# Attention, low-rank mixing and FFN on one core: batch 1's pooled attention result added inside the mixing, every fourth weight remainder on VectorE, raw weight chunks paced up to 16 ahead

## The chip, the cores and the metric

The kernel runs on one core of a Trainium2 chip. The metric is the device time of one execution in microseconds (us). Shown is the median of three runs, 1007.35 us (1007.11 to 1008.32). The profile is of a further execution, which took 1009.96 us.

## What is computed

Inputs q, k and v are 8 batches × 8 heads × 576 positions × 64, in f32 (the weights are f64). For each head two attentions are added, and the heads' results, side by side, are the x of a mixing and an FFN:

```python
q_d, k_d, v_d = (mean over groups of 4 positions)      # 144 pooled positions
out_up    = repeat(softmax(q_d k_d^T / 8) v_d, 4 times each)      # the pooled ("global") part
out_local = softmax(q k^T / 8, only where |i - j| < 4) v          # the local band
x  = (out_up + out_local), heads side by side          # 576 x 512 for each batch
u  = x + (x^T U V)^T                                   # U 576 x 32, V 32 x 576
out = u + relu(u w1) w2                                # w1 512 x 2048, w2 2048 x 512
```

## The kernel before

**A planner writes the order.** The code first only registers operations (class `Plan`): each has an engine, an estimated duration, the buffers that it reads and writes, and a priority. The planner then plays the schedule through with these estimates and emits the instructions in the order that came out. On the chip every engine runs its own list in that fixed order, and waits by semaphores where data is not there. All transfers are requested by SyncE (SP), also in that order: a request that has to wait holds up all those behind it. So a change of one cost or buffer can move instructions everywhere.

**Attention.** Work goes by batch (b) and head pair (hp), 4 pairs to a batch. Batch 0 has a form of its own at the start. For batches 1 to 7 (28 pairs), `late_global` makes the pooled part: scores, softmax, product with pooled v (`ps_a`, L571), scaled into `od` (L575; 112 rows × 3 × 64). It then stores `od` to `up_s` in DRAM, each row four times (L581, 6 transfers a pair). `local_attn` makes the band: its weights `ms`, products `Pt` of seven neighbours (GpSimd, L837); beside them, as the eighth addend, ScalarE copies the pooled part `ul` (L831), read back from `up_s` (L825); VectorE sums the eight (`acc`, L842); the sum is stored to `x_s` (L844).

**Mixing.** `mix_part` reads the pair's x back in two layouts: `xL` (positions on partitions, L890 and L893), and `Y` (L901), which VectorE transposes to `xT` (L906). ScalarE rounds `xL` to `xH` (L907), GpSimd makes the remainder `xL` (L908). TensorE multiplies with `Ust` (U in two parts) into `ps_hu` (L916). From that ScalarE and VectorE make `stk` (L920, L921, L924), which TensorE multiplies with `Vst` into `ps_u` (L723). VectorE adds it to `xT` (L727); ScalarE and GpSimd split the sum into a rounded part `uH` (L730) and a remainder `uL` (L732).

**FFN.** It goes by tiles of 288 positions (four, batches 0 and 1) and then 384; a tile of batch 1 can begin when all four pairs of that batch are mixed. A tile has 16 steps: 12 matmuls with w1 (`ps_h`, L941), relu split into `hH` (ScalarE, L949) and `hL` (VectorE, L950), and, three steps later, 12 matmuls with w2 into four accumulators (`acc`, L966). Steps before the 19th have only one PSUM bank for `ps_h`, so there a step waits for the `hL` of the one ahead. Steps of the FFN and attention's matmuls alternate on TensorE.

**Weights.** w1 and w2 come as 32 raw f64 chunks (512 KB each; `wr`, L414) and are converted by `convert`: ScalarE takes the upper 16 bits (`half`, L347), VectorE joins the bits (`y`, L350, in a PSUM bank; `c`, L352), ScalarE rounds to `W` (L358), GpSimd makes the remainder (L362). U and V go the same way with the remainder on VectorE (L366). Step 0 of the second product waits for the first 12 chunks (`NA`). The planner requests a chunk once the one `WD` = 4 earlier is converted.

Of the kernel before, what the change touches and what calls it, by code (L numbers as in the profile page):

```python
# [203 lines left out]
def attn_mix_ffn_kernel(ctx: ExitStack, tc, q, kp, vp, qT, kT, v, U, Ub, V, w1, w2, band, eye, pool, vw, ident, outT):  # L204
# [129 lines left out]
    nc.gpsimd.memset(Upool, 0.0)  # L334

    def convert(raw, pp, n, hi_out, lo_out, a, wkey, name, prio, own_bank=False, l0=0):
        t = buf(ffn, [128, CN], I32, name, "cT:" + name, 3)
# [12 lines left out]
        dve(n, lambda: nc.vector.tensor_scalar(  # L350
            out=yi(), in0=h().bitcast(I16)[:pp, :n], scalar1=65536.0, scalar2=None, op0=ALU.mult), [h, t], [y], prio)
        dve(1.15 * n, lambda: nc.vector.scalar_tensor_tensor(  # L352
            ti(), mid(), 13, yi(), op0=ALU.logical_shift_right, op1=ALU.bitwise_or), [raw, y], [t], prio)
# [4 lines left out]
        act(n, lambda: nc.scalar.activation(hi_out(), ta(), AF.Copy, scale=1.0 if big else 256.0), [t], own("H"), prio)  # L358
        if lo_out is None:
            return  # L360
        if big:
            pool_tt(1.0 * n, lambda: nc.gpsimd.tensor_tensor(  # L362
                out=lo_out(), in0=ta()[l0:], in1=hi_out()[l0:].bitcast(F32), op=ALU.subtract),
                [t, *own("H")], own("L"), prio)
        else:
            dve(n, lambda: nc.vector.scalar_tensor_tensor(  # L366
                lo_out(), ta()[l0:], 256.0, hi_out()[l0:].bitcast(F32), op0=ALU.mult, op1=ALU.subtract),
                [t, *own("H")], own("L"), prio)
# [433 lines left out]
    def local_attn(b, hp, up_s, x_s, s_s, prio):  # L802
# [22 lines left out]
        dma(lambda: nc.sync.dma_start(out=ul(), in_=up_s().rearrange("h (c s) d -> (h c) s d", s=NPOS)),  # L825
            [(up_s, 0), (up_s, 1)], [ul], prio + 0.2, 300)
        for p0 in range(0, NPOS, 2):
# [14 lines left out]
            dve(8.5 * n * D, lambda n=n, ps=ps, Pt=Pt: nc.vector.tensor_reduce(  # L842
                out=acc()[:, ps, :], in_=Pt()[:, :n], axis=AX.X, op=ALU.add), [(Pt, 0), (Pt, 1)], [(acc, p0)], prio)
# [245 lines left out]
```

## Time and profile before

| | before |
|---|---|
| median of 3 runs | 1007.35 us |
| profiled execution | 1009.96 us |
| its span, first to last instruction | 1008.2 us |
| mean granted TensorE clock | 0.990 |
| TensorE busy | 973.4 us (97%) |
| VectorE busy | 440.4 us (44%) |
| ScalarE busy | 349.6 us (35%) |
| GpSimd busy | 572.3 us (57%) |

In the rows of the profile PE is TensorE, PEld its weight loads, DVE VectorE, ACT ScalarE, POOL GpSimd and SPq SyncE's queue of requests. L941 is line 941 of the kernel before. A row of a timeline has the start, the duration, engine, line, operation and tiles (out<-in), and in brackets how long the engine had been idle and what ended that. A row of a group has the count, the total, and the mean in ns. The granted clock is 1.00 where TensorE runs at full speed.

### The profile page before, as it was taken

To read this page: it belongs to the slowest core of one execution; us is meant where nothing else is said; L and a number is where in the kernel's file an instruction comes from. 1 tells how busy PE (TensorE), PEld (TensorE's weight loads), DVE (VectorE), ACT (ScalarE), POOL (GpSimd) and SP (SyncE) were. 2 spreads that over 40 slices of the span, in tenths; PEclk is the share of its full clock that TensorE was granted. 3 is DMA by queue.
4 is the path that set the end of the run, shared out by engine and by line. 5 is a ranking of instruction groups with operands and counts; after the bars stand their busy time and mean duration, and the time that the engine had idled before them with its cause. 6 is when DMAs were issued, how large, how long until landed. Compare 5 with 4: busy or idle time off the path is not lost.

```text
span 1008.2 us, 24256 instructions
## 1 busy us (share of the span) xinstructions
PE 973.4 (97%) x9724; PEld 944.7 (94%) x9724; DVE 440.4 (44%) x824; ACT 349.6 (35%) x1023; POOL 572.3 (57%) x641
## 2 busy tenths in 40 slices
PE   5979999799999999999999999999999999999998
PEld 4769899799899999999999999999999999999998
DVE  5666855535453543642635444454363222211211
ACT  5766644333343333432433333433331221111110
POOL 6677897867766764864867866766764111300100
PEclk9989999989999999999999999999999999999999
DMA  9678867656564645655554565465541021000000
GB/s 280 170 243 228 260 147 152 142 129 159 108 152 105 171 92 124 147 129 125 147 129 104 145 150 127 111 161 123 123 121 54 13 68 24 32 1 1 32 1 31
DMA packets 220648, 120.01 MB, mean 119 GB/s; under 512 B 173988, under 2 KB 196856, under 8 KB 220536
## 3 DMA queue, kind: packets, MB, share of 16 engines
q1 hardware_dynamic: 220536, 118.47, 47.2%
q8 instruction: 76, 1.25, 0.5%
q14 instruction: 36, 0.29, 0.1%
HBM read 87.57 MB, written 30.86 MB: 117 GB/s over the span
## 4 chain that ended last, share of the span: by engine, by line
PE 80%; DMA 4%; POOL 4%; DVE 2%; issue 1%; SPq 1%; ACT 1%; DVEq 0%; POOLq 0%
PE ps_h L941 36%; PE acc L966 35%; PE ps_a L571 2%; POOL Pt L837 2%; PE ps_b L775 2%; PE ps_hu L916 2%; DMA ul<-up_s 1%; PE ps_t L556 1%; PE ps_b L768 1%; DMA s_s<-se 1%; DVE acc L842 1%; PE ps_u L723 1%; POOL W L362 1%; DMA gT<-in_kT 1%; SPq L791 1%
## 5 line engine op out<-in xcount | busy, mean ns | idle before, releaser
L966 PE MATMUL acc<-hH,W 128*128 128x384 f32 (+1 forms) x1664 | 441.9, 327 | 0.0
L941 PE MATMUL ps_h<-uH,W 128*128 128x384 f32 (+1 forms) x1376 | 360.4, 324 | 5.3 <-DVE hL L950 5.3
L966 PEld LDWEIGHTS acc<-hH,W 128*128 128x128 f32 x1664 | 297.4, 188 | 2.2
L966 PE MATMUL acc<-hL,W 128*128 128x384 f32 (+1 forms) x832 | 268.2, 322 | 0.0
L837 POOL TENSOR_TENSOR Pt<-vl,ms 128x896 f32<-128x896 f32 (+1 forms) x140 | 239.4, 1789 | 43.9 <-DMA vl<-in_vp 23.9
L950 DVE SCALAR_TENSOR_TENSOR hL<-ps_h,hH 128x384 fp32r<-128x384 f32 (+1 forms) x208 | 109.1, 524 | 342.6 <-ACT hH L949 342.6
L941 PEld LDWEIGHTS ps_h<-uH,W 128*128 128x128 f32 x1376 | 246.4, 190 | 7.5 <-DVE hL L950 6.3
L949 ACT ACTIVATE hH<-ps_h 128x384 fp32r<-128x384 f32 (+1 forms) x208 | 97.2, 467 | 378.3 <-PE ps_h L941 370.3
L941 PE MATMUL ps_h<-uL,W 128*128 128x384 f32 (+1 forms) x688 | 221.6, 322 | 1.4 <-POOL uL L732 1.4
L842 DVE TENSOR_REDUCE acc<-Pt 128x128 f32<-128x1024 f32 (+1 forms) x140 | 152.8, 1107 | 55.0 <-POOL Pt L837 28.0
L966 PEld LDWEIGHTS acc<-hL,W 128*128 128x128 f32 x832 | 156.7, 188 | 0.0
L941 PEld LDWEIGHTS ps_h<-uL,W 128*128 128x128 f32 x688 | 130.8, 190 | 1.6 <-POOL uL L732 1.6
L941 PE MATMUL ps_h<-u,W 128*128 128x384 f32 x432 | 98.1, 334 | 0.0
L831 ACT ACTIVATE Pt<-ul 128x128 f32<-128x128 f32 (+1 forms) x140 | 55.6, 432 | 92.6 <-DVE acc L842 61.7
L908 POOL TENSOR_TENSOR xL<-xL,xH 116x640 fp32r<-116x640 f32 x28 | 44.0, 1570 | 67.1 <-ACT xH L907 55.5
L732 POOL TENSOR_TENSOR uL<-xT,uH 128x384 fp32r<-128x384 f32 (+2 forms) x52 | 40.9, 808 | 68.4 <-ACT uH L730 66.1
L976 POOL TENSOR_TENSOR o<-uH,uL 128x384 f32<-128x384 f32 (+1 forms) x43 | 38.9, 938 | 70.0 <-DMA out_t<-o 70.0
L941 PEld LDWEIGHTS ps_h<-u,W 128*128 128x128 f32 x432 | 76.9, 188 | 0.0
L531 POOL TENSOR_TENSOR vr<-vr 72x256 f32<-72x256 f32 x56 | 41.4, 740 | 31.2 <-DMA vr<-in_v 31.1
L362 POOL TENSOR_TENSOR W<-c,W 128x512 fp32r<-128x512 f32 x32 | 41.1, 1287 | 14.5 <-ACT W L358 14.5
L727 DVE TENSOR_TENSOR xT<-ps_u,xT 128x384 f32<-128x384 f32 (+2 forms) x64 | 27.3, 450 | 32.1 <-PE ps_u L723 31.9
L775 PE MATMUL ps_b<-smk,smq 64*32 64x144 f32 x672 | 38.6, 294 | 0.4 <-POOL smk L439 0.4
(131 smaller groups left out, 903.3 us busy)
## 6 DMA issues: line engine op xcount, KB each, us to landing
wr<-in_W SPq DMA_DIRECT2D x32, 511.8 KB
vl<-in_vp SPq DMA_DIRECT2D x56, 240.0 KB
vr<-in_v SPq DMA_DIRECT2D x64, 144.0 KB
gT<-in_kT SPq DMA_DIRECT2D x28, 291.0 KB
gq<-in_qT SPq DMA_DIRECT2D x28, 288.0 KB
up_s<-od SPq DMA_DIRECT2D x168, 48.0 KB
ul<-up_s SPq DMA_DIRECT2D x28, 288.0 KB
x_s<-acc SPq DMA_DIRECT2D x28, 288.0 KB
```

The costliest lines, as they stand in the source:

```text
L362: pool_tt(1.0 * n, lambda: nc.gpsimd.tensor_tensor(out=lo_out(), in0=ta()[l0:], in1=hi_out()[l0:].bitcast(F32), op=ALU.subtract), [t, *own ...
L531: pool_tt(256, lambda x=x: nc.gpsimd.tensor_tensor(out=x()[:, :, 0:2, :], in0=x()[:, :, 0:2, :], in1=x()[:, :, 2:4, :], op=ALU.add), [x], ...
L732: pool_tt(n, lambda uH=uH, uL=uL, uf=uf, us=us: nc.gpsimd.tensor_tensor(out=uL.ap(hp, us), in0=uf(), in1=uH.ap(hp, us).bitcast(F32), op=AL ...
L775: nc.tensor.matmul(pg()[m:m + QL, a * SD:(a + 1) * SD], sq()[o, n:n + QL], sk()[o], start=True, stop=True)
L831: act(n * D, lambda n=n, ps=ps, Pt=Pt: nc.scalar.activation(Pt()[:, :n, :, 7], ul()[:, ps, :], AF.Copy), [ul], [(Pt, 1)], prio, 0.16)
L837: nc.gpsimd.tensor_tensor(out=Pt()[:, :n, :, 0:7].rearrange("p s d o -> p o s d"), in0=win, in1=at()[:, ps, :].rearrange("p s o -> p o s") ...
L842: dve(8.5 * n * D, lambda n=n, ps=ps, Pt=Pt: nc.vector.tensor_reduce(out=acc()[:, ps, :], in_=Pt()[:, :n], axis=AX.X, op=ALU.add), [(Pt, 0 ...
L908: pool_tt(640, lambda: nc.gpsimd.tensor_tensor(out=xL(), in0=xL().bitcast(F32), in1=xH().bitcast(F32), op=ALU.subtract), [xL, xH], [xL], prio)
L941: nc.tensor.matmul(ps()[:, :tn], W1[fc]()[:, w, dc, :], u.ap(dc), start=(n == 0), stop=(n == 3 * NDC - 1))
L949: last_h[i] = act(tn, lambda: nc.scalar.activation(hH()[:, :tn], ps()[:, :tn], AF.Relu), [ps], [hH], FIRST, 0.05)
L950: dve(tn, lambda: nc.vector.scalar_tensor_tensor(hL()[:, :tn], ps()[:, :tn], 0.0, hH()[:, :tn].bitcast(F32), op0=ALU.max, op1=ALU.subtract ...
L966: nc.tensor.matmul(ac[e]()[:, :tn], W2[fc]()[:, w, es], hx()[:, :tn], start=(fc == 0 and n == 0), stop=(fc == NFC - 1 and n == 2))
```

## The change

It has three parts, and the planner's order follows from them.

1. *Batch 1's pooled part.* For the four pairs of batch 1, `late_global` no longer stores `od`, and `local_attn` no longer reads `ul` nor copies it; its sums have seven addends. `mix_part` gets `od` (in two buffers that alternate) and adds it in the two places where x is used. Into `ps_hu` go six more f32 matmuls, `od` with a new constant `Upl` (U summed over groups of four positions). Six further f32 matmuls transpose `od` with the identity into free columns of the same bank (`oT`), and VectorE adds that to `xT`, each column four times (128 x 576), ahead of `stk`. `Upl` is made once by 12 small matmuls (`l_mm`) and two ScalarE copies.
2. *Remainders.* Of the 32 weight chunks every fourth has its remainder made by VectorE instead of GpSimd (8 chunks).
3. *Requests.* `WD` is 16 instead of 4, and chunk n gets an earliest time of 20 + 2.2 n us in the planner. That is no wait on the chip; it places the request in SyncE's list.

```diff
-    WD = 4
+    WD = 16
+    WAT, WAS = 20, 2.2
...
+    Upl = const.tile([128, 2, NQ, R], F32, name="Upl")
...
+    nc.gpsimd.memset(Upl, 0.0)
...
-        if big:
+        k = len(done) - 1
+        if big and not (k % 4 == 3):
             pool_tt(1.0 * n, lambda: nc.gpsimd.tensor_tensor(
...
-            dve(n, lambda: nc.vector.scalar_tensor_tensor(
-                lo_out(), ta()[l0:], 256.0, hi_out()[l0:].bitcast(F32), op0=ALU.mult, op1=ALU.subtract),
+            dve(1.15 * n, lambda: nc.vector.scalar_tensor_tensor(
+                lo_out(), ta()[l0:], 1.0 if big else 256.0, hi_out()[l0:].bitcast(F32), op0=ALU.mult, op1=ALU.subtract),
...
+        def l_mm():
+            for a in range(NQ):
+                for n, r in enumerate((3 * a // 2, 3 * a // 2 + 1)):
+                    for hh, m in enumerate((64, QC)):
+                        c = 64 - QL * r + QC * a
+                        nc.tensor.matmul(u3()[hh * 64:hh * 64 + m, a], pool_sb()[:, c:c + m], Ublk[:, r, 0:R],
+                                         start=(n == 0), stop=(n == 1))
+        op(PE, 1.0, l_mm, ["UbH", pool_sb], [pl], prio)
...
-            after=done[len(done) - WD:len(done) - WD + 1] if len(done) >= WD else ())
+            after=done[len(done) - WD:len(done) - WD + 1] if len(done) >= WD else (), at=WAT + WAS * len(done))
...
-        od = g([128, NQ, D], "od")
+        od = g([128, NQ, D], "od") if b > 1 or hp % 2 == 0 else buf(loc, [128, NPOS, D], F32, "ul")
...
+        if up_s is None:
+            return s_s, od
...
+        NO = 7 + (up_s is not None)
+        if up_s is not None:
+            ul = lb([128, NPOS, D], "ul")
+            dma(lambda: nc.sync.dma_start(out=ul(), in_=up_s().rearrange("h (c s) d -> (h c) s d", s=NPOS)),
...
-                out=acc()[:, ps, :], in_=Pt()[:, :n], axis=AX.X, op=ALU.add), [(Pt, 0), (Pt, 1)], [(acc, p0)], prio)
+                out=acc()[:, ps, :], in_=Pt()[:, :n, :, 0:NO], axis=AX.X, op=ALU.add), [(Pt, 0), (Pt, 1)], [(acc, p0)], prio)
...
+                for a in range(NQ if od is not None and i == 0 else 0):
+                    for hh in range(2):
+                        nc.tensor.matmul(ph()[:R, hh * D:(hh + 1) * D], Upl[:NP, hh, a], od()[:NP, a], start=False, stop=False)
+            if od is None:
+                return
+            for a in range(NQ):
+                for hh in range(2):
+                    o, m = slice(hh * 64, hh * 64 + QC), slice(hh * D, (hh + 1) * D)
+                    nc.tensor.matmul(oT()[m, a * QC:(a + 1) * QC], od()[o, a], ident_sb[o, o], start=True, stop=True)
...
+            dve(S, lambda: nc.vector.tensor_tensor(
+                out=xT().rearrange("p (j r) -> p j r", r=4), in0=xT().rearrange("p (j r) -> p j r", r=4),
+                in1=oT().unsqueeze(2).broadcast_to([128, SD, 4]), op=ALU.add), [ph, *xk], xk, prio)
...
-                up_s = buf(dram, [2, S, D], F32, "up_s", bufs=6)
+                up_s = buf(dram, [2, S, D], F32, "up_s", bufs=6) if b > 1 else None
```

How the order moves is shown at three places. The first is SyncE's list at the end of batch 1's last pair, before the change; `x_s_3105`, `xL_3189` and `Y_3248` are that pair's, `up_s_3081`, `vl`, `vr` and `ul_3187` belong to batch 2's first pair.

```order
L581 DMA up_s_3081<-od_3074 192x1x64 x3
L844 DMA x_s_3105<-acc_2964 128x576
L581 DMA up_s_3081<-od_3074 192x1x64 x3
L741 DMA vl_3135<-in_vp 64x960 x2
L529 DMA vr_3161<-in_v 72x2x256
L825 DMA ul_3187<-up_s_3081 128x576
L890 DMA xL_3189<-x_s_3105 112x2x320
L893 DMA xL_3189<-x_s_3105 4x2x320
L901 DMA Y_3248<-x_s_3105 32x18x32 x4
```

The same pair after the change (`x_s_3064`, `xL_3139`, `Y_3146`; the lines have moved by some 25):

```order
L764 DMA vl_3033<-in_vp 64x960 x2
L869 DMA x_s_3064<-acc_2865 128x576
L820 DMA sc_3071<-s_s_2957 128x9x7
L915 DMA xL_3139<-x_s_3064 112x2x320
L918 DMA xL_3139<-x_s_3064 4x2x320
L926 DMA Y_3146<-x_s_3064 32x18x32 x4
L604 DMA up_s_3237<-od_3231 192x1x64 x6
```

The loads of x now follow their store with one request between, and the next pair's `up_s` stands behind them. The second place is TensorE at the end of the first FFN tile: before, from the last matmul of step 31 of the second product on.

```order
L966 MATMUL acc3_2411<-hH_3318,W2_15_2269 128x288
L916 MATMUL ps_hu_3400<-xH_3380,Ust_82 64x128 x5
L916 MATMUL ps_hu_3400<-xL_3189,Ust_82 64x128 x5
L723 MATMUL ps_u_3433<-Vst_83,stk_3413 128x288
L723 MATMUL ps_u_3439<-Vst_83,stk_3413 128x288
```

After, from the same matmul on; `ul_2810` is the second of the two buffers that `od` uses.

```order
L1007 MATMUL acc3_2425<-hH_3219,W2_15_2090 128x288
L941 MATMUL ps_hu_3372<-xH_3322,Ust_82 64x128 x5
L945 MATMUL ps_hu_3372<-ul_2810,Upl_84 32x64 x6
L941 MATMUL ps_hu_3372<-xL_3139,Ust_82 64x128 x5
L951 MATMUL ps_hu_3372<-ident_sb_81,ul_2810 64x48 x6
L746 MATMUL ps_u_3409<-Vst_83,stk_3401 128x288
L746 MATMUL ps_u_3411<-Vst_83,stk_3401 128x288
```

The twelve new matmuls stand in the pair's `ps_hu`; the place of `ps_hu` and `ps_u`, next to each other behind step 31, is the same. The third place is VectorE where the FFN begins: before, from the twelfth chunk's join on (`y_a` and `y_h` are the same step in two banks; `hL_1204` is that of step 0, `hL_1295` that of step 1).

```order
L352 SCALAR_TENSOR_TENSOR c2_1115<-wr_1054,y_a_1145 128x512
L350 TENSOR_SCALAR y_h_1163<-half_1158 128x512
L352 SCALAR_TENSOR_TENSOR c1_1157<-wr_1086,y_h_1163 128x512
L350 TENSOR_SCALAR y_h_1192<-half_1170 128x512
L352 SCALAR_TENSOR_TENSOR c2_1169<-wr_1110,y_h_1192 128x512
L950 SCALAR_TENSOR_TENSOR hL_1204<-ps_h_1175,hH_1198 128x288
L350 TENSOR_SCALAR y_h_1236<-half_1224 128x512
L950 SCALAR_TENSOR_TENSOR hL_1295<-ps_h_1207,hH_1234 128x288
```

After (`hL_1207` is that of step 0, `hL_1264` that of step 1; L372 is a remainder on VectorE):

```order
L357 SCALAR_TENSOR_TENSOR c2_1174<-wr_1009,y_a_1195 128x512
L991 SCALAR_TENSOR_TENSOR hL_1207<-ps_h_1179,hH_1200 128x288
L355 TENSOR_SCALAR y_h_1225<-half_1203 128x512
L372 SCALAR_TENSOR_TENSOR W2_3_1210<-c2_1174,W2_3_1210 128x512
L357 SCALAR_TENSOR_TENSOR c1_1202<-wr_1067,y_h_1225 128x512
L355 TENSOR_SCALAR y_h_1252<-half_1237 128x512
L991 SCALAR_TENSOR_TENSOR hL_1264<-ps_h_1212,hH_1250 128x288
```

Two chunks' conversions that stood ahead of step 0's `hL` now stand behind it, with a remainder among them. Earlier in the same list, VectorE's first chunk conversion is its 17th instruction before and its 45th after: it has moved behind pair 1's attention, as the first requests for weights have moved behind the loads of q, k and v of batch 0 in SyncE's list.

More of the change, by code (lines that the diff above doesn't have):

```diff
@@ L264, in psum_pair, with dma @@
         return two
-    def dma(fn, r, w, prio, kb=295.0, issue=0.47, lat=1.3, after=()):
+    def dma(fn, r, w, prio, kb=295.0, issue=0.47, lat=1.3, after=(), at=0.0):
         late = (1.5 if r else 2.0) * (50 <= prio < 80) + 0.75 * (prio >= 80)
-        return op(SP, issue, fn, r, w, prio, after, move=0.01 + kb / 290.0, at=AT if prio >= 35 else 0.0, lat=lat + late)
+        return op(SP, issue, fn, r, w, prio, after, move=0.01 + kb / 290.0, at=max(at, AT if prio >= 35 else 0.0), lat=lat + late)
     def dve(n, fn, r, w, prio, two_x=False, after=()):
@@ L388, in load_ublk @@
         act(2 * R, lambda: nc.scalar.activation(Upool[:QH, :, 0:R], u4(), AF.Copy), [pu], ["Up"], prio, 0.16)
+        pl = psum(ps_acc, "ps_p", "acc1:p", 1)
+        u3 = lambda: pl()[:, :NQ * R].rearrange("p (a r) -> p a r", a=NQ)
+        def l_mm():
[7 more added lines that the diff above has]
+        for hh in range(2):
+            act(NQ * R, lambda o=slice(hh * 64, hh * 64 + QC), hh=hh: nc.scalar.activation(
+                Upl[o, hh], u3()[o], AF.Copy), [pl], [f"Ul{hh}"], prio, 0.16)
     def load_u(prio):
@@ L585, in late_global @@
             dma(lambda hh=hh: store(hh), [od], [(up_s, hh)], prio, 160, 1.3)
-        return s_s
+        return s_s, None
     def load_t(t, src, b, h0, prio):
@@ L830, in local_attn @@
             ps = slice(p0, p0 + n)
-            act(n * D, lambda n=n, ps=ps, Pt=Pt: nc.scalar.activation(
-                Pt()[:, :n, :, 7], ul()[:, ps, :], AF.Copy), [ul], [(Pt, 1)], prio, 0.16)
+            if up_s is not None:
+                act(n * D, lambda n=n, ps=ps, Pt=Pt: nc.scalar.activation(
+                    Pt()[:, :n, :, 7], ul()[:, ps, :], AF.Copy), [ul], [(Pt, 1)], prio, 0.16)
             def prod(p0=p0, n=n, ps=ps, Pt=Pt):
@@ L882, in u_of, with mix_part @@
         return u_bufs[ti]
-    def mix_part(b, hp, x_s, prio):
+    def mix_part(b, hp, x_s, od, prio):
         xL = buf(mix, [MP, 2, MJ, D], F32R, "xL")
@@ L917, in hu @@
                                      start=(i == 0 and j == 0), stop=(i == 1 and j == MJ - 1))
-        op(PE, 0.6, hu, [xH, xL, "UH", "UL"], [ph], prio, hold=HOLD * (b > 1))
+                for a in range(NQ if od is not None and i == 0 else 0):
[4 more added lines that the diff above has]
+            for a in range(NQ):
+                for hh in range(2):
+                    o, m = slice(hh * 64, hh * 64 + QC), slice(hh * D, (hh + 1) * D)
+                    nc.tensor.matmul(oT()[m, a * QC:(a + 1) * QC], od()[o, a], ident_sb[o, o], start=True, stop=True)
+        oT = lambda: ph()[:, 2 * D:2 * D + SD]
+        op(PE, 0.6 if od is None else 1.4, hu, [xH, xL, "UH", "UL"] + ([] if od is None else [od, "Ul0", "Ul1", "ident"]), [ph], prio,
+           hold=HOLD * (b > 1))
+        if od is not None:
+            xk = [(xT, t) for t in range(NT)]
+            dve(S, lambda: nc.vector.tensor_tensor(
+                out=xT().rearrange("p (j r) -> p j r", r=4), in0=xT().rearrange("p (j r) -> p j r", r=4),
+                in1=oT().unsqueeze(2).broadcast_to([128, SD, 4]), op=ALU.add), [ph, *xk], xk, prio)
         stk = buf(mix, [128, 2, D], F32R, "stk", bufs=2)
@@ L1002, in attention @@
             else:
-                up_s = buf(dram, [2, S, D], F32, "up_s", bufs=6)
+                up_s = buf(dram, [2, S, D], F32, "up_s", bufs=6) if b > 1 else None
                 x_s = buf(dram, [2, S, D], F32, "x_s", bufs=6)
-                s_s = late_global(b, hp, up_s, p - LEAD * (b == NE // HP))
+                s_s, od = late_global(b, hp, up_s, p - LEAD * (b == NE // HP))
                 local_attn(b, hp, up_s, x_s, s_s, p + 1)
-                mix_part(b, hp, x_s, p + 2)
+                mix_part(b, hp, x_s, od, p + 2)
     attention(0)
```

13 lines of the change are left out of this document (6 added, 7 removed).

## The prediction

> **What bounds the kernel now.** I read the core's span and clock first, then engine time by stretch.
>
> ```profile
> core 0: 1008.2 us, clock 0.990
> ...
> 0.00:60.00 60.00, 45.40 (x866) 37.69 (x866) 38.23 (x94) 38.19 (x121) 37.02 (x55) 0.97 0.78 232
> 60.00:199.00 139.00, 127.95 (x1550) 123.19 (x1548) 86.52 (x160) 72.33 (x200) 115.36 (x129) 0.98 0.76 192
> 199.00:1008.20 809.20, 800.08 (x7312) 783.83 (x7310) 315.67 (x571) 239.04 (x703) 419.90 (x459) 0.99 0.41 98
> ...
> 60.00:66.00 6.00, 2.79 (x16) 1.98 (x14) 5.54 (x11) 5.43 (x12) 5.29 (x9) 1.00 0.48 157
> 66.00:73.00 7.00, 5.29 (x51) 5.00 (x52) 3.21 (x6) 2.28 (x5) 6.58 (x11) 0.51 1.02 306
> ...
> 199.00:209.50 10.50, 7.27 (x48) 6.74 (x47) 3.99 (x9) 2.22 (x7) 10.34 (x14) 0.51 0.55 153
> ```
>
> After each stretch's length come the busy microseconds of TensorE, its weight loads, VectorE, ScalarE and GpSimd, then the granted TensorE clock. The last long stretch has TensorE busy for 800.08 of 809.20 us: a change can bring little there. The idle time is in the first two: 14.6 us (60 − 45.40) before the FFN, 11.05 us (139 − 127.95) up to 199. Beside it there is slow time: from 66 to 73 and from 199 to 209.5 the granted clock is 0.51, so of 5.29 and 7.27 us of work 49% is lost, 2.6 and 3.6 us. What TensorE waits for is in its table of waits (total, times, longest):
>
> ```profile
> PE ps_h L941 <- DVE hL L950: 5.3, 4, 2.2
> ...
> PE ps_u L723 <- DVE stk L921: 2.9, 1, 2.9
> ...
> PE ps_hu L916 <- POOL xL L908: 2.6, 1, 2.6
> PE ps_t L556 <- DVE xT L727: 2.3, 1, 2.3
> ```
>
> The second and third row are one place: the end of the first FFN tile, where TensorE comes to the mixing of batch 1's last pair. The chain of waits and the SyncE queue tell why it is late.
>
> ```profile
> 185.65 0.32 ACT hH L949
> 185.96 4.33 DMA ul<-up_s
> ...
> 191.07 2.25 POOL uL L732 x3
> ...
> 193.38 3.75 POOL Pt L837 x2
> 197.13 1.40 POOL xL L908
> 198.53 1.79 POOL Pt L837
> ...
> 200.34 1.23 DVE acc L842
> ...
> 201.59 0.28 DVE stk L921
> ```
>
> ```profile
> 180.56 0.59 SPq L844 DMA_DIRECT2D x_s<-acc  x1
> 181.19 1.86 SPq L581 DMA_DIRECT2D up_s<-od  x3
> ...
> 185.96 0.35 SPq L825 DMA_DIRECT2D ul<-up_s  x1
> 186.40 0.38 SPq L890 DMA_DIRECT2D xL<-x_s  x1
> ...
> 187.23 2.54 SPq L901 DMA_DIRECT2D Y<-x_s  x4
> ```
>
> The pair's local result leaves at 180.56, but its way back (xL, Y) is issued only at 186.40, behind the next pair's `up_s` stores and the `ul` load that had to wait for them. That load is in at 190.3 (185.96 + 4.33), and ScalarE's copies of it stand ahead of its `uH`; GpSimd's `uL` and two `Pt` come after that, and only then `xL` at 197.13. TensorE waits 2.6 us for that and 2.9 us for `stk`, which stands on VectorE behind an `acc` of 1.23 us. With the slow clock after it, this one place costs 2.6 + 2.9 + 3.6 = 9.1 us.
>
> The other cluster is the start of the FFN (TensorE, then VectorE):
>
> ```profile
> 64.99 0.41 PE L941 MATMUL ps_h<-uL,W 128*128 128x288 f32 x1 [1.38 <-POOL uL L732]
> 65.23 0.29 PE L941 MATMUL ps_h<-uH,W 128*128 128x288 f32 x1
> 67.71 0.61 PE L941 MATMUL ps_h<-uH,W 128*128 128x288 f32 x1 [2.19 <-DVE hL L950]
> ```
>
> ```profile
> 65.02 0.69 DVE L352 SCALAR_TENSOR_TENSOR c<-wr,y_h 128x512 int32<-128x512 int32 x1
> 65.81 0.69 DVE L350 TENSOR_SCALAR y_h<-half 128x512 int32<-128x512 int16 x1
> 66.60 0.69 DVE L352 SCALAR_TENSOR_TENSOR c<-wr,y_h 128x512 int32<-128x512 int32 x1
> 67.20 0.45 DVE L950 SCALAR_TENSOR_TENSOR hL<-ps_h,hH 128x288 fp32r<-128x288 f32 x1
> ```
>
> Step 1 waits 2.19 us for `hL` of step 0, which stands on VectorE behind conversions of two chunks that nothing needs yet.
>
> **The change part by part.** The remaining prices stand in these rows (timeline rows: start, duration; grouped rows: total, mean ns):
>
> ```profile
> 83.12 0.91 PE L571 MATMUL ps_a<-vs,E 72*64 72x64 f32 x24
> ...
> L385 PE MATMUL ps_p<-Ublk,pool 128*72 128x32 f32 x12 | 1.7, 309 | 0.0
> ...
> L362 POOL TENSOR_TENSOR W<-c,W 128x512 fp32r<-128x512 f32 x32 | 41.1, 1287 | 14.5 <-ACT W L358 14.5
> ...
> L696 DVE TENSOR_TENSOR xT<-ps_x,oT 128x512 f32<-128x512 f32 x4 | 2.7, 685 | 0.9 <-PE ps_x L693 0.9
> ...
> 21.43 0.46 DVE L366 SCALAR_TENSOR_TENSOR Vst<-cv,Vst 32x288 fp32r<-32x288 f32 x1
> ...
> 24.06 1.46 DVE L366 SCALAR_TENSOR_TENSOR Vst<-cv,Vst 32x288 fp32r<-32x288 f32 x1
> ...
> 23.94 1.26 POOL L454 TENSOR_TENSOR vr<-vr 72x512 f32<-72x512 f32 x1
> ```
>
> *The pooled result in the mixing.* TensorE gets 12 small f32 matmuls for each of batch 1's four pairs. Twelve f32 matmuls with 64 moving columns (24 records) took 0.91 us, so 4 × 0.91 = 3.6 us; the new twelve are somewhat narrower or as wide, hence 2.5 to 4. The constant `Upl` costs 12 small matmuls once; the nearest row took 1.7 us for 12 records, so 0.8 to 1.7 us, of which I take 0.9, since TensorE idles a quarter of that stretch anyway. TensorE is the bound, so **+4.5 us** (3 to 6) stands against the change. ScalarE loses 20 copies and SyncE 24 stores and 4 loads, all off the path except where named. VectorE gets four adds of 128x576: 0.685 × 576/512 = 0.77 us each. Three lie beside FFN matmuls, but the fourth does not: at the end of the tile TensorE has nothing between the pair's `ps_hu` and `ps_u`, and the add stands ahead of `stk`.
>
> In return the chain above is cut. For pair 3 the SyncE queue has `x_s`, one small load, `xL`, `Y`, and the next pair's `up_s` only after them; VectorE has no `acc` of the next pair ahead of `stk`. GpSimd still has three `uL` and a `Pt` ahead of `xL`, but the copies of `ul` which set their start are gone for this batch. How soon the loads can follow their store no row shows; the `ul` load stood 2.9 us behind the end of its own stores' issue (181.19 + 1.86 to 185.96) with other loads between, so `xL` can go out between 181.2 and 184.1, 2.3 to 5.2 us earlier, against a wait of 2.6 us. I take the middle, and for the doubt leave 0.5 us of that wait. The second wait becomes the add, `stk` and the hops between engines, 0.77 + 0.28 + 0.3 = 1.35 us in place of 2.9 (0.3 is an estimate: several hops of 0.02 to 0.06 us between the chain's rows, and `ps_hu` itself). With 1.85 us idle I expect the clock to hold, as it did over the 2.3 us before `ps_t`: **−7.2 us** (−9.1 to 0; 0 if `xL` is as late as before).
>
> [...]
>
> *The start of the FFN.* In the new order step 0's `hL` stands right behind the twelfth chunk's conversion and no longer behind two more. Then the wait of 2.19 us falls to `hH` and `hL` with their hops, 0.32 + 0.45 + 0.1 = 0.9: −1.3 us. With 1.38 + 0.9 = 2.3 us idle the clock should hold too, −2.6 us. Against this, VectorE's conversions begin later (requests no longer go out ahead of the attention's loads), and it has 38.23 us of work in the first 60; two of its remainders now stand ahead of the FFN, 2 × 0.69 by the `c` row. I take +1 us for it. Together **−2.9 us**, from −8 (the early waits for inputs shrink as well) to +5 (the twelfth chunk is late).
>
> *Every fourth remainder on VectorE.* GpSimd sheds 8 × 1.287 = 10.3 us, hidden mostly, since it is late at the tile's end alone. VectorE gets 8 × 0.69 = 5.5 us if nothing is in the way. But the same kind of instruction with both inputs in SBUF took 0.46 us with GpSimd idle, and 1.46 beside GpSimd's reading of `vr`: 1.0 us lost. So 8 more us are possible, and 13.5 in all if each delays an `hL` by its whole length; 0 if all lie under matmuls. Two or three stand within two rows of an `hL`, so I take **+1 us**, near the low end.
>
> [...]
>
> *The rest.* The 2.3 us before `ps_t` later in batch 2 may fall apart in the new order: **−0.4** (−2.3 to 0). The other `hL` waits (5.3 − 2.2 = 3.1 us) come from `acc` reductions ahead of `hL`; seven addends in place of eight shorten them a little: 0.
>
> Sum: +4.5 − 7.2 − 2.9 + 1 − 0.4 = −5.0 us.
>
> **The rivals.**
> 1. *The tile's end stays as it is* (slower). In both orders `ps_hu` of the last pair stands right behind step 31, and GpSimd, busy 115.36 of 139 us, has three `uL` and a `Pt` ahead of `xL`. If `xL` is as late as now, the 7.2 us are not won: −5.0 + 7.2 = +2.2 us, and with the longer add ahead of `stk` 0.8 more and another 0.5 of half clock, +3.5. [...] For it: only the planner's costs say that GpSimd is free in time. Against it: `xL` itself can be loaded 2.3 to 5.2 us earlier. Time 1007.35 + 3.5 = 1011.
> 2. *VectorE pays* (about no change). Later conversions and blocked remainders delay the twelfth chunk or `hL` by 5 us: −5.0 + 5 = 0, 1007.5. For it: 1.46 against 0.46, and the paced requests still stand in SyncE's fixed order behind `vw` loads that wait for TensorE. Against: VectorE is idle a third of the time.
> 3. *The start gains more.* Attention's first loads no longer share the transfers with weights, the 14.6 idle us lose 5 more: −10, 997.
> 4. *The order's reshuffle cancels*: what is won at the tile's end is waited for at the next `ps_u`; within the same bounds as 2.
>
> **How the numbers follow.** The profiled execution took 1009.96 us (span 1008.2), 2.6 above the median of 1007.35; the sum is a difference, so it is taken from the median: 1007.35 − 5.0 = **1002.3 us**. Chances: forecast 0.50 (998 to 1005), rival 1 0.20, rivals 2 and 4 0.15, rival 3 0.15 (992 to 998). For 8 in 10 I leave out the far tail of rival 3 and of rival 1: 992 to 1011. About 0.2%, 2 us, can be told from no change. Faster by more: 0.50 + 0.15 and a little of rival 2, 0.67; within: 0.13; slower: rival 1, 0.20.
>
> **What would show it.** Right: no wait of `ps_hu` on `xL` over 1 us, at the first tile's end a wait of 1 to 2 us for `stk`, granted clock near 1.00 in that stretch, 12 new records' groups of about 0.9 us in four places; step 1's wait for `hL` near 1 us. Wrong in the part on VectorE: remainders of 1.3 us or more with `hL` behind them. Wrong altogether: the half clock at the first tile's end still there, or FFN step 0 starting later than 65 us.

## The result, and the profile after

The changed kernel took 1017.46 us (median of 11 runs, 1014.97 to 1023.03), the kernel before 1009.77 us in the 11 runs beside them. The ratio is 1.0094, 95% interval 1.0074 to 1.0114: slower by 0.9%, where 0.5% faster had been forecast. The profiled execution took 1014.97 us, the fastest of the eleven, so it shows less of the loss than the median has.

A tile has 16 steps, so step 31 is the last step of the second tile: what is called the end of the first FFN tile above is the end of batch 0's two tiles. Here it is called the end of step 31, and what lies behind it begins with step 32, the first that needs batch 1.

From the changed kernel's profile: the engines' busy time, then its stretches (length, busy microseconds of TensorE, weight loads, VectorE, ScalarE, GpSimd, then the clock); the last row runs from the start of step 32 to TensorE's end.

```profile
PE 978.6 (97%) x9844; PEld 946.9 (93%) x9844; DVE 447.5 (44%) x836; ACT 342.0 (34%) x1005; POOL 565.3 (56%) x634
```

```profile
0.00:60.00 60.00, 44.41 (x892) 36.10 (x893) 38.72 (x95) 38.20 (x123) 34.60 (x53) 0.97 0.78 241
60.00:199.00 139.00, 132.53 (x1626) 127.42 (x1624) 92.02 (x166) 65.21 (x172) 107.11 (x121) 0.98 0.61 163
...
203.50:1009.00 805.50, 799.27 (x7310) 781.61 (x7308) 314.19 (x571) 237.21 (x706) 421.37 (x456) 1.00 0.41 98
```

TensorE is busy for 978.6 us instead of 973.4, and between 60 and 199 it idles 6.5 us instead of 11.05. Behind step 31 it idles 6.2 us (805.50 − 799.27), and there the kernel before has 2.5 (800.20 − 797.71); its row between the same two points is

```profile
204.60:1004.80 800.20, 797.71 (x7286) 781.97 (x7284) 311.89 (x563) 237.23 (x697) 414.46 (x451) 1.00 0.41 97
```

So 4.5 us of idle are won between 60 and 199, 1.0 is lost before 60 (15.6 against 14.6) and 3.7 behind step 31, and TensorE is busy 5.2 us longer: +5.4, against 5.0 between the two spans (1013.2 and 1008.2). TensorE's waits in the changed kernel:

```profile
PE ps_h L982 <- DVE hL L991: 5.4, 4, 2.3
PE ps_a L590 <- POOL vs L553: 4.1, 3, 2.0
...
PE ps_h L982 <- POOL uL L755: 2.6, 2, 1.4
PE ps_u L746 <- DVE stk L962: 1.8, 1, 1.8
```

The wait for `xL` at the end of step 31 is gone. In its place stand waits for `vs` (the pooled v, made by GpSimd from the load `vr`) and for `uL`, also made by GpSimd. The end of step 31 in the changed kernel, on TensorE, VectorE, ScalarE and GpSimd:

```profile
197.43 0.47 PE L941 MATMUL ps_hu<-xH,Ust 116*64 116x128 f32 x5
197.83 0.86 PE L945 MATMUL ps_hu<-ul,Upl 112*32 112x64 f32 x12
198.62 0.51 PE L941 MATMUL ps_hu<-xL,Ust 116*64 116x128 f32 x5
199.06 0.55 PE L951 MATMUL ps_hu<-ident_sb,ul 48*64 48x48 f32 x12
201.37 0.54 PE L746 MATMUL ps_u<-Vst,stk 128*128 128x288 f32 x2 [1.75 <-DVE stk L962]
...
207.05 0.40 PE L982 MATMUL ps_h<-uL,W 128*128 128x288 f32 x1 [1.24 <-POOL uL L755]
```

```profile
199.66 0.75 DVE L957 TENSOR_TENSOR xT<-xT,ps_hu 128x576 f32<-128x576 f32 x1 [1.42 <-PE ps_hu L951]
...
201.03 0.28 DVE L962 TENSOR_TENSOR stk<-ps_hu,stk 32x128 fp32r<-32x128 f32 x1 [0.61 <-ACT stk L965]
```

```profile
200.45 0.27 ACT L961 ACTIVATE stk<-ps_hu 64x128 fp32r<-64x128 f32 x1 [2.95 <-DVE xT L957]
200.73 0.27 ACT L965 ACTIVATE stk<-ps_hu 32x128 fp32r<-32x128 f32 x1
```

```profile
204.99 0.74 POOL L551 TENSOR_TENSOR vr<-vr 72x256 f32<-72x256 f32 x1 [2.58 <-DMA vr<-in_v]
205.80 0.45 POOL L553 TENSOR_TENSOR vs<-vr 72x128 f32<-72x128 f32 x1
206.21 1.55 POOL L755 TENSOR_TENSOR uL<-xT,uH 128x288 fp32r<-128x288 f32 x2
```

`xL` is in time. The new add reads the same bank as ScalarE's first `stk` copy, and that copy is released by the add's end (200.41 to 200.45; the row's bracket names it), so add, two copies and `stk` stand one behind the other: 1.75 us. Then comes a wait that the forecast did not have: GpSimd's `uL` stands behind a `vr` that waits 2.58 us for its load, and TensorE waits 1.24 us for `uL`.

### The profile page after: what moved, and what is told of

It is laid out like the page before. It is cut to its first block, busy times and chain, and to the rows that moved or that the text cites. A ratio compares the mean times of both kernels' runs of the same rounds, so it can differ in the third digit from the quotient of the medians.

```text
span 1013.2 us, 24443 instructions
## 1 busy us (share of the span) xinstructions
PE 978.6 (97%) x9844; PEld 946.9 (93%) x9844; DVE 447.5 (44%) x836; ACT 342.0 (34%) x1005; POOL 565.3 (56%) x634
## 4 chain that ended last, share of the span: by engine, by line
PE 55%; POOL 1%; DMA 1%; SPq 1%; issue 0%; DVE 0%; ACT 0%; DVEq 0%; POOLq 0%
PE acc L1007 25%; PE ps_h L982 25%; PE ps_a L590 1%; POOL Pt L862 1%; PE ps_b L797 1%; PE ps_hu L941 1%; PE ps_t L576 1%; PE ps_b L790 1%; DMA vl<-in_vp 1%; DMA ul<-up_s 1%; SPq L604 0%; PE ps_u L746 0%; SPq L813 0%; DVE o L1020 0%; POOL vr L551 0%
## 5 line engine op out<-in xcount | busy, mean ns | idle before, releaser
L867 DVE TENSOR_REDUCE acc<-Pt 128x128 f32<-128x1024 f32 (+3 forms) x140 | 150.0, 1089 | 66.0 <-ACT Pt L856 25.2
L856 ACT ACTIVATE Pt<-ul 128x128 f32<-128x128 f32 (+1 forms) x120 | 47.4, 434 | 117.1 <-DVE acc L867 64.8
L368 POOL TENSOR_TENSOR W<-c,W 128x512 fp32r<-128x512 f32 x24 | 30.9, 1292 | 13.0 <-ACT W L363 12.8
```

The source lines that it names most:

```text
L856: act(n * D, lambda n=n, ps=ps, Pt=Pt: nc.scalar.activation(Pt()[:, :n, :, 7], ul()[:, ps, :], AF.Copy), [ul], [(Pt, 1)], prio, 0.16)
L867: dve((NO + 0.5) * n * D, lambda n=n, ps=ps, Pt=Pt: nc.vector.tensor_reduce(out=acc()[:, ps, :], in_=Pt()[:, :n, :, 0:NO], axis=AX.X, op=A ...
```

## The experiments

The times of one comparison are from one chip; each ratio is to the kernel before, run in turns beside it, and the parentheses hold its 95% interval. These are the ratios of the seventeen variants that were timed against it, and TensorE's idle time from the start of step 32 to its end (length less busy time of that stretch, one profile each):

| parts | other number | ratio | idle behind step 31, us |
|---|---|---|---|
| 1 | | 0.999 (0.996 to 1.002) | 1.2 |
| 2 | | 0.995 (0.993 to 0.997) | 1.2 |
| 3 | | 0.991 (0.989 to 0.994) | 3.0 |
| 1, 2 | | 1.003 (1.000 to 1.006) | 5.6 |
| 1, 3 | | 1.000 (0.998 to 1.002) | 6.6 |
| 2, 3 | | 0.996 (0.993 to 0.998) | 2.9 |
| 1, 2, 3 again | | 1.009 (1.006 to 1.012) | 9.0 |
| 1, 2, 3 | new matmuls twice | 1.012 (1.008 to 1.016) | 6.9 |
| 1, 2, 3 | pace 2.0 | 1.000 (0.998 to 1.002) | 0.6 |
| 1, 2, 3 | pace 2.1 | 1.008 (1.005 to 1.011) | 5.8 |
| 1, 2, 3 | pace 2.3 | 0.996 (0.993 to 0.998) | 1.9 |
| 1, 2, 3 | pace 2.4 | 0.997 (0.995 to 1.000) | 0.3 |
| 1, 2, 3 | hold 1.7 | 1.011 (1.008 to 1.014) | 8.4 |
| 1, 2, 3 | hold 1.4 | 1.011 (1.008 to 1.015) | 9.4 |
| none | hold 1.6 | 1.002 (1.000 to 1.004) | 3.6 |
| none | hold 1.4 | 1.001 (0.998 to 1.004) | 3.1 |
| 3 | pace 2.4 | 0.996 (0.994 to 0.999) | 2.0 |

Where only some parts are in, the planner's cost of 1.15 n for the remainders of U and V stays as in the changed kernel. Where nothing stands in the second column, the pace (the 2.2 of part 3) is 2.2 and the hold 1.5. The hold is a number of the planner that keeps back the matmuls of a mixing, from batch 2 on. The kernel before has 2.5 and 3.8 us in its two profiles.

**Each part alone.** The theory after the result was W: TensorE's new work is the loss. Its rivals were V (the remainders), P (the pace) and R (the planner's new order).

```diff
-    WD = 16
+    WD = 4                          # in the changed kernel: only part 1 is left
...
-        if big and not (k % 4 == 3):
+        if big:
...
-            after=done[len(done) - WD:len(done) - WD + 1] if len(done) >= WD else (), at=WAT + WAS * len(done))
+            after=done[len(done) - WD:len(done) - WD + 1] if len(done) >= WD else ())
```

> Only the first part: batch 1's pooled result in the mixing; remainders all on GpSimd, requests as before. Theory W (the loss is TensorE's own new work, 1.3 us in each of the four mixings of the changed profile, 5.2 us in all, of which the first tile's end gives back 2 to 4): 1 to 4 us slower than before, idle at the first tile's end under 4 us. Theory V (the loss is the eight remainders on VectorE): 0 to 4 us faster than before. Theory P (the loss is the paced requests): the same, 0 to 4 us faster.

Measured: 0.999, no difference; the 1 to 4 us of W did not come. TensorE does the new work of the mixing here too, so in this order about as much is given back.

```diff
-        if big:
+        if big and not (k % 4 == 3):      # in the kernel before, with the cost of 1.15 n: only part 2
```

> Only the second part: every fourth chunk's remainder on VectorE. Theory V: 4 to 8 us slower than before, with remainders of over 1 us standing right ahead of an hL that TensorE waits for. Theories W and P: within 2 us of before; the first tile's end keeps its two waits of 2.6 and 2.9 us.

Measured: 0.995, a gain of 5 us that none of the theories had. V falls for this part by itself. At the end of step 31 the wait for `stk` stays at 2.9 us, and that for `xL` is 1.1.

```diff
-    WD = 4
+    WD = 16                         # in the kernel before: only part 3
+    WAT, WAS = 20, 2.2
...
+            ..., at=WAT + WAS * len(done))
```

> Only the third part: 16 chunks ahead at the fixed pace. Theory P: 4 to 8 us slower than before, with the FFN's first steps waiting for chunks. Theories W and V: within 2 us of before, the FFN's first step starting 1 to 2 us earlier as in the changed kernel.

Measured: 0.991. P falls too, and this gain was expected by none either.

The changed kernel as it is:

> The changed kernel once more beside the three parts, on the same chip: 7 to 11 us slower than before. If the three parts' differences add up to it, the parts act by themselves; if not (theory R: the planner's new order elsewhere makes the loss), the difference that is left is the reordering, and waits behind GpSimd in batches 2 to 5 stand in this profile too.

Measured: 1.009 again. The parts do not add up: 0.999, 0.995 and 0.991 would make 0.985. The difference of 2.4%, 24 us, shows in no part alone. Each of these ratios is that of one order, though, and so are those of the pairs; how far the order by itself moves the time is measured below. The waits behind GpSimd stand in this profile too (3.9 us for `uL`, 2.5 for `vs`). Its span is 1026.4 us at a clock of 0.973, that of the first profile 1013.2 at 0.993.

**Pairs.**

```diff
-    WD = 16
+    WD = 4        # in the changed kernel, and without at=...: parts 1 and 2
```

> Parts 1 and 2 together, requests as before. Each part alone stood at 0.999 and 0.995 of before. Theory A (the parts add up, and only all three together fall into a bad order): 0.990 to 0.998. Theory G (GpSimd and VectorE's remainders meet the shortened chain of batch 1, so parts 1 and 2 hurt each other): 1.005 to 1.015, with waits of TensorE behind GpSimd in batches 2 to 5.

Measured: 1.003, between the two theories' ranges.

```diff
-        if big and not (k % 4 == 3):
+        if big:        # in the changed kernel: parts 1 and 3
```

> Parts 1 and 3 together, remainders on GpSimd. Alone they stood at 0.999 and 0.991. Theory A: 0.985 to 0.995. Theory T (pooled mixing and pacing hurt each other: the loads of batch 2 meet the weights): 1.005 to 1.015.

Measured: 1.000, again between.

```diff
-                up_s = buf(dram, [2, S, D], F32, "up_s", bufs=6) if b > 1 else None
+                up_s = buf(dram, [2, S, D], F32, "up_s", bufs=6)        # in the changed kernel, and without Upl: parts 2 and 3
...
```

> Parts 2 and 3 together, batch 1 as before. Alone they stood at 0.995 and 0.991. Theory A: 0.983 to 0.991. Theory V (remainders on VectorE are harmful once the chunks come at the pace, since they then stand ahead of the first hL): 1.002 to 1.01.

Measured: 0.996, between. So every pair loses against the sum of its parts, and neither A nor a quarrel of one certain pair describes it. Part 1 costs 0.8 to 0.9% on top of part 2 or 3 (0.995 to 1.003, 0.991 to 1.000) and 1.3% on top of both, though nothing alone.

The kernel before as it is:

> The kernel before once more, for a second profile: the same idle time of TensorE (about 31 us with the start and the end) and the same two waits at the first tile's end. If the slow clock comes with those waits alone, it covers the same stretches as in the first profile, some 20 us; if it comes by chance at waits of 1 to 3 us, other stretches, and the span differs by its length.

A single run: 1010.16 us, a span of 1008.4, and the two waits at the end of step 31 are there with 3.0 and 2.6 us. Besides 195 to 206 the slow clock covers 264 to 267 here, after a wait of 3.1 us, where the first profile's wait of 2.3 us was followed by none; before the FFN it covers 55 to 59 instead of 49 to 53. So the slow stretches are not the same, and do not come with those two waits alone. The last section shows what they follow.

**Is it the new work or the order?** Twice the matmuls keeps the order; another pace keeps the work.

```diff
-                for a in range(NQ if od is not None and i == 0 else 0):
+                for a in 2 * list(range(NQ if od is not None and i == 0 else 0)):
...
-            for a in range(NQ):
+            for a in 2 * list(range(NQ)):
```

> The changed kernel with its twelve new matmuls of each mixing issued twice, the planner's cost for them as it was, so that every engine's order stays the same (the product with Upl is then added twice, so batch 1's output is wrong by one pooled term in the mixing). Theory W (TensorE's new work is paid in full): 5 us slower than the changed kernel, ratio to before 1.013 to 1.016. Theory R (the loss is in the new order's waits, and there is slack for some work): within 2 us of the changed kernel, 1.008 to 1.011.

Measured: 1.012 (1.008 to 1.016), against 1.009 (1.006 to 1.012) for the changed kernel. The intervals overlap, so this does not part the theories: the second 5 us could be paid in full or half hidden.

```diff
-    WAT, WAS = 20, 2.2
+    WAT, WAS = 20, 2.0
```

> The changed kernel with the pace at 2.0 instead of 2.2 us a chunk. That is a number of the planner alone; the work is the same to the instruction, only its order differs. Theory R (the order is drawn anew by any small change, and the changed kernel drew a bad one): a time of its own, over 3 us away from the changed kernel. Theory W: within 2 us of the changed kernel, 1.007 to 1.011.

```diff
-    WAT, WAS = 20, 2.2
+    WAT, WAS = 20, 2.4
```

> The changed kernel with the pace at 2.4 us a chunk, again the same work in another order. Theory R: over 3 us away from the changed kernel, and not on a line with the pace of 2.0. Theory W: within 2 us of the changed kernel.

Measured: 1.000 and 0.997. The same instructions in another order take 9 to 12 us less than the changed kernel. That is theory R, and W by itself falls: the work is in all three. The stretch behind step 31 at a pace of 2.4:

```profile
199.20:996.70 797.50, 797.24 (x7327) 781.28 (x7314) 317.29 (x573) 240.72 (x715) 420.83 (x459) 1.00 0.42 100
```

TensorE idles 0.26 us there instead of 6.2. The other five orders of the same work, same stretch: at a pace of 2.0, 2.1 and 2.3, and with the hold at 1.7 and 1.4.

```profile
207.40:1003.00 795.60, 794.95 (x7190) 779.40 (x7188) 316.17 (x567) 237.93 (x702) 415.92 (x450) 1.00 0.41 98
```

```profile
208.60:1011.80 803.20, 797.44 (x7189) 779.48 (x7188) 312.69 (x567) 234.18 (x700) 415.80 (x450) 1.00 0.42 97
```

```profile
206.30:1006.20 799.90, 798.02 (x7288) 780.72 (x7284) 315.98 (x570) 237.18 (x704) 421.87 (x456) 1.00 0.42 98
```

```profile
205.50:1017.10 811.60, 803.19 (x7310) 783.52 (x7308) 315.91 (x571) 237.86 (x706) 418.60 (x456) 0.99 0.42 97
```

```profile
207.00:1018.80 811.80, 802.37 (x7311) 783.54 (x7308) 314.54 (x571) 236.28 (x707) 420.05 (x456) 0.99 0.42 97
```

The idle time behind step 31 parts these orders: 0.3, 0.6 and 1.9 us where the ratio is 1.000 or less, 5.8 to 9.4 where it is 1.008 or more. The slow clock comes on top: in this stretch it is at half for 0 to 3.4 us in the three good orders and for 1.2 to 24 us in the bad ones. The idle time does not rank kernels of different content (parts 1 and 3 idle 6.6 us there at 1.000).

```diff
-    HOLD = 1.5
+    HOLD = 1.6        # in the kernel before
```

> The kernel before with the planner's hold of a mixing's matmuls at 1.6 instead of 1.5 us: same work, another order from batch 2 on. Theory R: 2 us or more from before, to either side. Theory W: within 2 us of before, 0.998 to 1.002.

Measured: 1.002 (1.000 to 1.004), which lies on the border between the two and decides nothing.

**How wide do the orders scatter?**

```diff
-    WAT, WAS = 20, 2.2
+    WAT, WAS = 20, 2.1
```

> The changed kernel at a pace of 2.1. Theory R (draws of the order scatter by some 5 us around a content that is worth nothing or little): 0.994 to 1.006. Theory W (the content itself costs, and 2.0 and 2.4 were lucky): 1.006 to 1.012.

```diff
-    WAT, WAS = 20, 2.2
+    WAT, WAS = 20, 2.3
```

> The changed kernel at a pace of 2.3. Theory R: 0.994 to 1.006, and TensorE's waits behind the first tile (GpSimd's uL and vs) shorter than in the changed kernel. Theory W: 1.006 to 1.012.

Measured: 1.008 at 2.1, which is W's range, and 0.996 at 2.3, which is R's, with 1.9 us of idle behind step 31 as R had it. So the five paces give 1.000, 1.008, 1.009, 0.996, 0.997. That looks like two groups some 1% apart rather than R's scatter about one value, but five orders are few. Their plain mean is 1.002.

```diff
-    HOLD = 1.5
+    HOLD = 1.4        # in the kernel before
```

> The kernel before with the hold at 1.4: same work, another order from batch 2 on. Theory R: within 5 us of before to either side, 0.995 to 1.005. Theory W: within 2 us, 0.998 to 1.002.

Measured: 1.001. With 1.000 and 1.002 the kernel before scatters little when only its later part is drawn anew.

```diff
-    WAT, WAS = 20, 2.2
+    WAT, WAS = 20, 2.4        # in part 3 alone
```

> The third part alone at a pace of 2.4 instead of 2.2. Theory R: its 0.991 was partly a draw, now 0.993 to 1.003. Against it (pacing itself is worth the 9 us): 0.988 to 0.993.

Measured: 0.996 against 0.991 at 2.2: the intervals just touch. By the two ratios about half of the part's gain was the order's, and both orders are faster than before.

**Where in the order is it?** The last two keep the first part of the changed kernel's order: up to 240 us (hold 1.7) and 370 us (hold 1.4) the lists of VectorE, ScalarE, GpSimd and SyncE are the same in the profiles.

```diff
-    HOLD = 1.5
+    HOLD = 1.7
```

> The changed kernel with the planner's hold at 1.7 instead of 1.5: TensorE's order is the same until batch 1's last pair is mixed (the first tile's end), and another one behind it. Theory L (the loss is in the waits behind the first tile): the idle there under 3 us, 0.997 to 1.004. Theory S (the loss is in the start and the first tile): 1.006 to 1.012 as in the changed kernel.

```diff
-    HOLD = 1.5
+    HOLD = 1.4
```

> The changed kernel with the hold at 1.4: TensorE's order is the same until batch 3's first pair is mixed, some 350 us in, and another one behind it. Theory L: the waits right behind the first tile stay and those in batches 3 to 6 are drawn anew, 1.000 to 1.008. Theory S: 1.006 to 1.012.

Measured: 1.011 and 1.011. As a number this is theory S. But the idle time behind step 31 did not go; it is 8.4 and 9.4 us. With the hold at 1.7 the longest waits are

```profile
PE ps_h L982 <- DVE hL L991: 5.0, 3, 2.3
PE ps_a L590 <- POOL vs L553: 3.7, 2, 2.7
PE ps_h L982 <- POOL uL L755: 3.4, 2, 2.0
```

again `vs` and `uL`. So new draws of the later order did not help, which speaks for something inherited from the first part, though two draws do not prove it. One row of the profiles does part the good orders from the bad ones, the wait for `vs`. At paces of 2.0, 2.1, 2.3 and 2.4 it is

```profile
PE ps_a L590 <- POOL vs L553: 0.6, 1, 0.6
```

```profile
PE ps_a L590 <- POOL vs L553: 3.4, 4, 1.7
```

```profile
PE ps_a L590 <- POOL vs L553: 1.1, 2, 0.9
```

```profile
PE ps_a L590 <- POOL vs L553: 0.2, 1, 0.2
```

and in the five profiles at 2.2 with all three parts (one has the matmuls twice) 2.5 to 5.5 us. Why `vs` is late differs from place to place. In the changed kernel's longest such wait, GpSimd comes from a run of `Pt`:

```profile
421.76 8.25 POOL L862 TENSOR_TENSOR Pt<-vl,ms 128x896 f32<-128x896 f32 x5 [0.44 <-DMA vl<-in_vp]
429.88 0.74 POOL L551 TENSOR_TENSOR vr<-vr 72x256 f32<-72x256 f32 x1
...
430.82 0.47 POOL L553 TENSOR_TENSOR vs<-vr 72x128 f32<-72x128 f32 x1
```

```profile
431.35 0.87 PE L590 MATMUL ps_a<-vs,E 72*48 72x64 f32 x22 [1.97 <-POOL vs L553]
```

At a pace of 2.1 GpSimd waits 3.1 us for the load of `vr` ahead of the longest one. These waits are a part of the loss, not all of it. What certainly belongs to the shared first part is the wait for `uL` right behind step 31: it is 1.2 to 2.5 us in all five profiles at 2.2, but the other bad pace, 2.1, does not have it, nor do the good ones. The two fastest orders, 2.3 and 2.4, also differ at the end of step 31: 15 of the second product's matmuls, step 31's among them, stand between the last pair's `ps_hu` and its `ps_u`, and TensorE does not wait for `stk` at all. What in the first part makes `vs` late afterwards stays open.

## Why the prediction was wrong

**The step that failed** is the last of the sum, "the rest", with rival 4: the new order outside the three places was priced at 0 to −2.3 us, as if it could only take waits away, and rival 4 ("what is won at the tile's end is waited for at the next `ps_u`") was held within no change. The runs showed new waits of TensorE there, for `vs` and `uL`: 6.2 us of idle behind step 31 against 2.5. Between paces of 2.1 or 2.2 and of 2.0, 2.3 or 2.4, with the same work, the order is worth 0.8 to 1.4%, 8 to 14 us. The range had no term for that. Which step of the planner makes the bad orders is not known. The named terms were too hopeful as well: with the sizes of this one profile, worked out below, they come to about nothing (6.1 − 4.4 − 1.9 us) instead of −5.0.

**The end of step 31.** The mechanism was right: the wait for `xL` is gone, and the wait for `stk` is 1.75 us against 1.35 forecast, because ScalarE's two copies stand between the add and `stk`. Missed was the next thing late, `uL` behind a `vr` whose load was requested at 202.23, and the clock did fall: it is 0.81 from 196 to 205.2 where 1.00 was forecast.

```profile
202.23 0.36 SPq L549 DMA_DIRECT2D vr<-in_v  x1
```

```profile
196.00:205.20 9.20, 7.04 (x62) 6.28 (x61) 3.58 (x9) 2.78 (x12) 4.39 (x7) 0.81 0.74 179
```

Of the 9.1 us that the place cost, 1.75 + 0.41 (a wait for `xT` ahead of the next matmuls) + 1.24 = 3.4 us of idle are still there, and 7.04 × 19% = 1.3 us of clock. The gain was about 4.4 us, not 7.2, and only in this profile. In the second profile of the same kernel the wait for `uL` is 2.48 us, and half clock covers 13.7 us there:

```profile
206.40:220.10 13.70, 11.22 (x65) 10.47 (x64) 6.55 (x11) 3.88 (x12) 8.43 (x10) 0.50 0.34 75
```

There the place costs 1.75 + 2.48 + 11.22 × 50% = 9.8 us, and nothing was won. The prediction had named half clock at this place as a sign of being wrong altogether, and it is there in both.

**TensorE's new work.** Forecast 4.5 us. By the rows above the twelve matmuls of one mixing take 0.8 + 0.5 us (from start to start, 197.83 to 198.62, and 199.06 to some 199.6) where 0.9 had been taken; four times that and some 0.9 us for `Upl` are 6.1. TensorE's busy time rose by 5.2, but busy time holds the slow clock as well: at a pace of 2.4 the same work is busy for 972.2 us, less than the kernel before.

**The FFN's start.** Forecast −2.9. In this profile the first step begins 1.9 us earlier (60.0 against 61.9), but that is chance: the four other profiles whose order is the same up to there have it at 62.3 to 65.1, and the three others of the kernel before (two with another hold) at 60.1 to 60.3. In the median it begins some 3 us later in the changed kernel; why is not known, and the good orders begin no earlier (59.2 to 65.2). The wait of 2.2 us for `hL` is as it was, 2.27 in all five. TensorE, and VectorE ahead of that `hL`:

```profile
63.08 0.40 PE L982 MATMUL ps_h<-uL,W 128*128 128x288 f32 x1 [1.39 <-POOL uL L755]
65.87 0.61 PE L982 MATMUL ps_h<-uH,W 128*128 128x288 f32 x1 [2.27 <-DVE hL L991]
```

```profile
63.19 0.69 DVE L357 SCALAR_TENSOR_TENSOR c<-wr,y_a 128x512 int32<-128x512 int32 x1
63.98 0.70 DVE L355 TENSOR_SCALAR y_a<-half 128x512 int32<-128x512 int16 x1
64.76 0.69 DVE L357 SCALAR_TENSOR_TENSOR c<-wr,y_a 128x512 int32<-128x512 int32 x1
65.37 0.45 DVE L991 SCALAR_TENSOR_TENSOR hL<-ps_h,hH 128x288 fp32r<-128x288 f32 x1
```

The order was read rightly, `hL` right behind the twelfth chunk; wrong was that this chunk would be done by then. Its conversion began later (its last step at 64.76 against 63.58) and ends, counted from step 0's start, as late as the fourteenth's did before: 5.4 us behind it (64.76 + 0.69 − 60.0, and 66.60 + 0.69 − 61.9).

**The remainders.** Forecast +1, with 0 to 13.5 as bounds. Alone the part is faster (0.995). In the changed kernel six of the eight take 0.68 to 0.93 us, two take 3.4 and 3.1. VectorE, GpSimd and TensorE around the first of these:

```profile
107.44 3.38 DVE L372 SCALAR_TENSOR_TENSOR W<-c,W 128x512 fp32r<-128x512 f32 x1
110.74 0.44 DVE L991 SCALAR_TENSOR_TENSOR hL<-ps_h,hH 128x288 fp32r<-128x288 f32 x1
```

```profile
105.41 1.32 POOL L368 TENSOR_TENSOR W<-c,W 128x512 fp32r<-128x512 f32 x1
106.66 3.73 POOL L862 TENSOR_TENSOR Pt<-vl,ms 128x896 f32<-128x896 f32 x2
```

```profile
111.24 0.40 PE L982 MATMUL ps_h<-uH,W 128*128 128x288 f32 x1 [1.74 <-DVE hL L991]
```

The remainder ends 0.4 us behind the second of two `Pt`, and TensorE waits 1.74 us for the `hL` behind it. The other long one ran from 119.68 to 122.76, beside five instructions of GpSimd in a row that ended at 122.20. The four that ran while GpSimd was idle took 0.68 to 0.69 us, and two that ran beside two instructions of GpSimd each (0.4 and 0.9 us) took 0.74 and 0.93. So what was lost was lost beside GpSimd's work, 2.4 and 2.7 us in the two long ones; why some lose that much and others almost nothing was not shown. The kernel before waits 1.36 us for an `hL` near that place, so the net price was small, as forecast.

**The clock.** The prediction counted half clock in the kernel before at two places, 66 to 73 and 199 to 209.5, and expected the clock to hold over 1.85 us of idle because it had held over 2.3 us before `ps_t`. Half clock stands there from 49.1 to 52.5 too, and the wait before `ps_t` left TensorE 46% busy in its step (1.58 of 3.42 us):

```profile
49.10:52.50 3.40, 3.40 (x16) 3.07 (x16) 1.23 (x4) 2.99 (x10) 1.37 (x2) 0.50 0.97 287
264.12:267.54 3.42, 1.58 (x13) 1.58 (x14) 3.42 (x6) 1.09 (x4) 3.42 (x6) 1.00 0.64 53
```

So these places were too few to read a rule from; the last section has more. No run shows the 0.5 us of further half clock in rival 1's sum; at the end of step 31 the clock cost 1.3 us in one profile of the changed kernel and 5.6 (11.22 × 50%) in the other.

## What to carry to other kernels

Where a planner sets the order, a change has two effects: its own, which can be worked out place by place, and a new draw of the order everywhere else. Here the second was some 1%, more than the 0.5% that the first was thought to be worth, so a change of that size is judged by several draws (a planner's number moved a little, with the work the same) and not by one. Among these draws, pacing alone gave 0.991 and 0.996, and all three parts at a pace of 2.3 gave 0.996: all are faster than before, and the changed kernel was one of the two bad paces out of five. The same holds for profiles: the start of the first FFN step lies anywhere from 60.0 to 65.1 us in five profiles of one order, so a difference of 2 us between two profiles is no finding. Not tried: `stk` ahead of the new add on VectorE, which would take the add out of the 1.75 us, and an order that is made to keep matmuls between `ps_hu` and `ps_u`, as it came out at 2.3 and 2.4.

## What the runs showed of the hardware

TensorE's clock fell after a shorter wait than the 1.85 us over which the prediction expected it to hold. In the run with the hold at 1.4 one wait of 1.77 us was followed by 3.4 us at half clock; in the changed kernel the same wait of 1.74 us was not. Within one profile all changes of the granted clock lie a whole number of steps of 3.41 us apart (in the changed kernel at 54.99, 58.41, 65.23, 72.06, 201.77 and 205.18), and where these steps lie differs from execution to execution (half clock begins at 201.77 in one profile of the changed kernel and at 206.4 in the other, 1.4 steps later). So what is compared here is how much of a wait falls into one step. Hold 1.4, then the changed kernel, the step that holds most of the wait and the next one:

```profile
111.94:115.35 3.41, 1.64 (x13) 1.41 (x12) 3.41 (x3) 0.00 (x0) 2.26 (x2) 1.00 0.00 0
115.35:118.76 3.41, 3.41 (x16) 3.41 (x16) 3.03 (x5) 1.28 (x3) 2.42 (x3) 0.50 0.00 0
```

```profile
109.61:113.02 3.41, 1.78 (x13) 1.78 (x14) 3.41 (x5) 0.63 (x1) 1.28 (x2) 1.00 0.00 0
113.02:116.44 3.42, 3.42 (x28) 3.42 (x27) 3.42 (x7) 1.62 (x3) 3.42 (x5) 1.00 0.06 11
```

TensorE was busy for 48% and 52% of the two steps. Over all twenty profiles, between 66 and 990 us: of the steps at full clock, 24 were busy for less than 46%, and half clock followed each of them; of 71 that were busy for 46 to 76%, half clock followed 17; of 5244 busier ones, none. In the first profiles of the two kernels alone these are 1 of 1, 1 of 10 and none of 521. (The ends of matmuls are modelled, so these shares are rough.)

So a step need not be idle throughout for half clock to follow: with the hold at 1.4 one that was idle for 52% was enough, one of the 17 above. What sets those 17 apart from the other 54 was not shown.

What this is worth: the two profiles of the changed kernel have spans of 1013.2 and 1026.4 us, and TensorE idles 34.6 and 34.9 us in them. Nearly the whole difference is busy time, 978.6 against 991.5 us; the clock is at half for 13.7 us in the one and 55 in the other.
